# Handing two batches between DFT stages through DRAM in place of transposes on chip

## The chip, the cores and the metric

The kernel runs on one NeuronCore of one Trainium2 chip. The metric is the time of one execution on the device, in microseconds (us). The engines are PE (matmul), DVE (vector), ACT (scalar) and POOL (GpSimd); SP issues most DMAs and computes nothing. Each engine works through its own instructions in program order, and so does SP's DMA queue: an instruction that waits holds up everything behind it on its engine.

## What is computed

The reference mixes tokens with a filter in the frequency domain, and sends every token through one of eight two-layer experts, chosen by a hash of its id:

```python
# x: (8, 2496, 256) f32; filt_r, filt_i: (1249, 256)
X = np.fft.rfft(x, axis=1)
Y = X * (filt_r + 1j * filt_i)[None]
x = np.fft.irfft(Y, n=2496, axis=1).astype(np.float32).reshape(19968, 256)

expert_idx = token_ids * np.int64(2654435761) % np.int64(8)
for e in range(8):                       # w1: (8, 256, 1024), w2: (8, 1024, 256)
    mask = expert_idx == e
    out[mask] = np.maximum(x[mask] @ w1[e], 0.0) @ w2[e]
```

## The kernel before

**Two halves that overlap.** The eight batches go through a DFT written as matmuls, in three stages. The filtered tokens are scattered, row by row, to the table `xs` in DRAM, where each expert's tokens lie together in tiles of 256. The expert half then takes tile after tile from `xs`: `load` fetches one, `up` multiplies by `w1`, `down` by `w2`, and `store` scatters the results to the output. The tiles are ordered by the batches that they need. The first tiles hold tokens of batches 0 and 1 alone, so the expert half can begin when these two batches (`first` and `second` in the code) are in `xs`. All that is done ahead of the first tile is called the head here. The other six batches are worked in between the tiles.

**The three stages.** 2496 points are split into 39 x 64. `stage1` does the short DFT. `forward` and `back` are stage 2: `forward(u)` multiplies two of the 20 frequencies s by the table `d_t` on PE, and DVE applies the filter to the result (four passes, L318 to L323); `back(u)` multiplies by `e_t`. There are N_2 = 10 steps u. `stage3(u)` does the short inverse DFT for up to four columns j of the result (NU = 6 steps), has ACT copy the rows to a buffer `o`, and has POOL scatter them with one indirect DMA per column, 22 for each batch (L433). `room(u)` takes an `o` buffer and writes the token numbers into it on DVE; there are four such buffers for the first two batches, and one comes free when its scatters have landed.

**How data gets from stage to stage.** Stage 3 needs the data with other indices on the partitions than stage 2 leaves them. Batches 2 to 7 go through a tile in DRAM: `back` writes, `load4` reads. Batches 0 and 1 stay on chip. For them `back_c` takes the place of `back`: it exchanges the operands of the matmul, so that the result has channels on the partitions, kept in `self.out`. `turn4(u)` then transposes it with the identity matrix on PE (44 transposes for a batch, 84 of full size in both) into PSUM banks a to d, and ACT (first) or DVE (second) copies them to the tile `t4` that `stage3` reads. `t4` tiles come from a pool of two, eight columns each (index v = u // 2).

**Where things lie.** `self.out` of first is a part of `wts`, the buffer that later holds the weights of the expert tiles; `self.out` of second is a part of `mid`. The stage-1 results of fourth (batch 3) go to the same part of `mid`. `third` is batch 2. The tiles of x for stage 1 come from a pool of two, `xpool`.

**What sets the order.** The order of the head is written out by hand. `head` is a list of pairs (number, piece); sorted by the number, it gives the order in which the pieces are issued. The numbers resemble microseconds but act as keys only: each engine, and SP, receives its part of every piece in that order. In `chain(k)`, first's stage 2 runs as turn2 (towards stage 2), back and forward. Second's own steps of stage 2 have the keys 62.7 + 2.9 u. `weights(i, which)` loads the weights of tile i on SP, `load1` the x tiles, `load2` the inputs of stage 2. At its end, `begin()` frees the buffers of the head, and `load(0)` and `load(1)` fetch the first tiles; they wait for the scatters of batches 0 and 1. Fourth's first four steps of stage 1 have keys just below these (123 to 123.3).

The pieces' keys before, as far as the change touches them:

```python
    at = (63, 68.6, 74.4, 80.2, 86, 91)
    head += [(t, lambda u=u: first.turn4(u)) for u, t in enumerate(at)]
    head += [(t + 3, lambda u=u: first.stage3(u)) for u, t in enumerate(at)]
    head += [(96 + 5 * u - 4 * (u > 0), lambda u=u: second.turn4(u)) for u in range(NU)]
    head += [(98 + 5 * u, lambda u=u: second.stage3(u)) for u in range(NU)]
```

Of the kernel before, what the change touches and what calls it, by code (L numbers as in the profile page):

```python
# [19 lines left out]
P = 128  # L20
# [105 lines left out]
def kernel(  # L126
# [92 lines left out]
    class Batch:  # L219


        def __init__(self, b):
            self.b = b
            self.d1 = self.d2 = None
            self.x, self.t2, self.t4, self.p, self.o = {}, {}, {}, {}, {}
            self.g = None
            if b < 2:

                if b == 0:
                    own = mid[:, 0:5, :].rearrange("p k f -> p (k f)")  # L230
                    self.mixed = own.rearrange("p (h n s) -> p h n s", h=2, s=NS)
                after = (held[:, 0:NS * C] if b == 0 else mid[:, 5:10, :].rearrange("p k f -> p (k f)"))
                self.out = after.rearrange("p (h n s) -> p h n s", h=2, s=NS)

# [18 lines left out]
        def products(self, w, rows, cols, src, dst, copy, u, name):  # L253
# [3 lines left out]
            for i in range(1 if last else XG // 2):  # L257
                ps = fps.tile([P, 2, C], F32, name=f"{name}_{self.b}_{u}_{i}", tag="f")
                if last:
# [112 lines left out]

        def back_c(self, u):
            pr = self.p.pop(u)
            ps = fps.tile([P, 2, 2, P], F32, name=f"pc_{self.b}_{u}", tag="f")
            for i in range(2):
                for h in range(2):
                    nc.tensor.matmul(out=ps[:, i, h, :], lhsT=pr[:, i, h * P:(h + 1) * P],
                                     rhs=e_t[:, 2 * u + i, :], start=True, stop=True)
            nc.scalar.copy(out=self.out[:, :, :, 2 * u:2 * u + 2], in_=ps[:].rearrange("p i h n -> p h n i"))  # L380

        def turn4(self, u):
            v, j0 = divmod(XG * u, XL)
            if j0 == 0:
                self.t4[v] = t4pool.tile([NK, XL, C], F32, name=f"t4_{self.b}_{v}", tag="t4")
            copy = nc.vector.tensor_copy if self.b else nc.scalar.copy
            for k in range(0, min(XG, HN + 1 - XG * u), 2):
                tag = ("bc" if self.b and u % 2 else "ad")[k // 2]
                ps = banks[tag].tile([P, 2, C], F32, name=f"pu_{self.b}_{u}_{k}", tag=tag)
                rows = [2 * NS * (H if XG * u + k + i < HN else 1) for i in range(2)]  # L390
                for i in range(2):
                    n0 = 2 * H * (XG * u + k + i)
                    for h in range(2):
                        nc.tensor.transpose(out=ps[0:rows[i], i, h * P:(h + 1) * P],
                                            in_=self.out[:, h].rearrange("p n s -> p (n s)")[:, n0 * NS:n0 * NS + rows[i]],
                                            identity=ident[:])
                if rows[0] == rows[1]:
                    copy(out=self.t4[v][:, j0 + k:j0 + k + 2, :], in_=ps[0:NK])
                else:
                    for i in range(2):  # L400
                        copy(out=self.t4[v][0:rows[i], j0 + k + i, :], in_=ps[0:rows[i], i, :])

# [348 lines left out]
    def chain(k):  # L751

        for step, j in ((Batch.turn2, k + 1), (Batch.back_c, k - 2), (Batch.forward, k)):
            if 0 <= j < N_2:
# [23 lines left out]
    head += [(62.7 + 2.9 * u, lambda u=u: second.forward(u)) for u in range(N_2)]  # L778
    head += [(62.7 + 2.9 * (u + 2) - .1, lambda u=u: second.back_c(u)) for u in range(N_2)]
    at = (63, 68.6, 74.4, 80.2, 86, 91)  # L780
    head += [(t, lambda u=u: first.room(u)) for u, t in enumerate((60, 65, 71, 77, 83, 88.5))]
    head += [(t, lambda u=u: second.room(u)) for u, t in enumerate((92, 96.9, 101.9, 106.9, 111.9, 116.9))]
    head += [(t, lambda u=u: first.turn4(u)) for u, t in enumerate(at)]
    head += [(t + 3, lambda u=u: first.stage3(u)) for u, t in enumerate(at)]
    head += [(t, lambda v=v: third.load1(v)) for v, t in enumerate((72, 73, 74))]
    head += [(t, lambda k=k: weights(k // 2, k % 2)) for k, t in enumerate((95, 95.1, 95.2, 95.3))]
    head += [(96 + 5 * u - 4 * (u > 0), lambda u=u: second.turn4(u)) for u in range(NU)]
    head += [(98 + 5 * u, lambda u=u: second.stage3(u)) for u in range(NU)]
    head += [(99 + 5 * u - 3 * (u == 5), lambda u=u: third.stage1(u)) for u in range(NU)]
    head += [(123.5, lambda: begin()), (123.6, lambda: [load(i) for i in range(2)])]  # L790
# [340 lines left out]
```

## Time and profile before

| What | Value |
|---|---|
| time of the kernel, median of 3 runs (lowest, highest) | 1452.11 us (1450.68, 1458.1) |
| the profiled execution: its time, its span | 1424.24 us, 1422.5 us |
| its mean granted PE clock | 0.99 |
| busy over the span: PE, DVE, ACT, POOL | 97%, 63%, 29%, 58% |
| first matmul of the first expert tile (`up_a`) starts at | 141.85 us |
| scatters of first and second start, from the first to the last | 69.97 us to 135.26 us |
| bytes moved by DMA over the span | 278.33 MB |

The profile is of one execution, which was shorter than the timed runs; times within the kernel are measured from the start of its span. A line of the timeline gives start, duration, engine, line, operation, output <- input, the count of merged instructions, and in brackets how long the engine was idle before and what ended that. A line of the chain of waits gives start, duration, and what that stretch was spent in. Lines of the code are named by L and their number; a line of a helper stands for all who call it, so L267 is the matmuls of stages 1 (`pa`) and 3 (`pd`), and L433 is every scatter to `xs`. In names, `pc` is the result of `back`, `pb` of `forward`, `pu` of `turn4`.

In the head the engines are less full than over the span. In the windows of the trace, from 60 to 80 us PE is busy 15.91 us, DVE 15.76, ACT 7.26 and POOL 5.92; from 100 to 120 us PE 19.22, DVE 6.89, ACT 10.03 and POOL 15.07. The DMA engines' share is 0.66 and 0.95.

### The profile page before, as it was taken

The numbers are of one execution on the slowest core, as the hardware profiler recorded it, in microseconds if no ns is written. First come the engines' busy times: TensorE is split into PE (matmuls) and PEld (weight loads), VectorE is DVE, ScalarE is ACT, GpSimd is POOL, SyncE is SP. The second block draws the span as 40 slices with busy tenths as digits, with TensorE's granted clock in tenths as the row PEclk, the third lists the DMA queues.
The fourth block names the chain that finished last, engine by engine and source line by source line (L and its number), as shares of the span: only waits on it lengthen the run. The fifth ranks groups of instructions, "written<-read, shape, count | busy, mean of one in ns | idle before, by whom it ended". The sixth has DMA issues, their size and how long they took to land.

```text
span 1422.5 us, 26307 instructions
## 1 busy us (share of the span) xinstructions
PE 1373.4 (97%) x9398; PEld 1273.3 (90%) x9398; DVE 890.2 (63%) x1636; ACT 416.6 (29%) x760; POOL 830.3 (58%) x736
## 2 busy tenths in 40 slices
PE   7898999999999999999999999999999999999997
PEld 7776888989888988889999899999999999999997
DVE  7773575575556566445665477657766776676775
ACT  4554122223232223232222222222222222222222
POOL 6167243844665565578533587788855566555563
PEclk9999899999999999999999999999999999999999
DMA  8677765757987698888755785887742526261611
GB/s 222 206 235 216 212 218 121 260 192 245 269 270 224 183 284 264 261 262 273 241 167 131 219 258 170 235 242 235 254 138 68 190 62 199 46 218 42 215 46 35
DMA packets 244505, 278.33 MB, mean 196 GB/s; under 512 B 125171, under 2 KB 213670, under 8 KB 234948
## 3 DMA queue, kind: packets, MB, share of 16 engines
q1 hardware_dynamic: 95149, 179.33, 40.2%
q10 hardware_dynamic: 129303, 52.69, 15.4%
q0 software_dynamic: 19920, 44.59, 8.9%
q8 instruction: 77, 1.26, 0.4%
q14 instruction: 56, 0.46, 0.1%
HBM read 293.65 MB, written 86.15 MB: 267 GB/s over the span
## 4 chain that ended last, share of the span: by engine, by line
PE 86%; DMA 8%; DVE 3%; issue 1%; ACT 1%; ACTq 0%; SPq 0%; POOLq 0%; POOL 0%; DVEq 0%
PE dps L922 22%; PE up_b L887 9%; PE up_a L887 6%; PE up_c L887 6%; PE pd L267 5%; PE pb L312 4%; PE dnc L949 4%; PE dnb L949 4%; PE dna L949 4%; PE upc L944 4%; PE upa L944 4%; PE pc L335 3%; PE pa L267 3%; DMA t<-d 2%; PE upe L944 2%; PE upb L944 2%
## 5 line engine op out<-in xcount | busy, mean ns | idle before, releaser
L922 PE MATMUL dps<-wts,ht 128*128 128x256 f32 x1600 | 370.9, 382 | 6.1 <-ACT ht L891 6.1
L922 PEld LDWEIGHTS dps<-wts,ht 128*128 128x128 f32 x1600 | 304.7, 192 | 50.6 <-ACT ht L891 7.3
L1014 POOL DMA_INDIRECT out_dram<-osb,no x158 | 165.2, 1046 | 219.2 <-DVE osb L956 137.8
L433 POOL DMA_INDIRECT xs<-o,sidx x176 | 177.0, 1006 | 168.7 <-ACT o L269 73.3
L877 POOL TENSOR_TENSOR tw<-wts 128x512 f32<-128x512 f32 x158 | 205.1, 1298 | 116.0 <-DMA wts<-in_moe_w_dram 92.4
L877 POOL TENSOR_TENSOR tw<-wts,tw 128x512 f32<-128x512 f32 x158 | 206.1, 1305 | 6.2
L894 DVE TENSOR_TENSOR ht<-up_b,ht 128x512 f32<-128x512 f32 x150 | 103.7, 691 | 114.6 <-PE up_b L887 91.2
L891 ACT ACTIVATE ht<-ht 128x512 f32<-128x512 f32 x150 | 94.3, 630 | 188.8 <-DVE ht L894 164.9
L322 DVE TENSOR_TENSOR z<-pb,filt 64x512 f32<-64x512 f32 x160 | 110.2, 689 | 30.9 <-PE pc L335 28.9
L927 DVE COPY osb<-dps 128x512 f32<-128x512 f32 x50 | 34.6, 691 | 150.2 <-PE dps L922 149.7
L887 PE MATMUL up_a<-xt,wts 128*128 128x128 f32 x800 | 115.3, 277 | 9.1 <-DVE xt L855 4.9
L887 PEld LDWEIGHTS up_a<-xt,wts 128*128 128x128 f32 x800 | 105.9, 193 | 12.7 <-DVE xt L855 5.3
L887 PE MATMUL up_b<-st,tw 128*128 128x128 f32 x800 | 107.4, 278 | 2.7 <-DVE ht L894 1.8
L887 PEld LDWEIGHTS up_b<-st,tw 128*128 128x128 f32 x800 | 98.1, 193 | 4.9 <-issue 3.7
L953 ACT ACTIVATE ht<-ht 128x512 f32<-128x512 f32 x90 | 56.6, 630 | 122.1 <-DVE ht L956 75.8
L894 DVE TENSOR_TENSOR ht<-up_c,ht 128x512 f32<-128x512 f32 x100 | 69.0, 690 | 37.2 <-PE up_c L887 32.4
L338 ACT COPY mid<-pc 128x512 f32<-128x512 f32 x60 | 35.0, 584 | 154.8 <-PE pc L335 91.5
L267 PE MATMUL pd<-t,wi_t 120*117 120x256 f32 x320 | 77.5, 385 | 2.6 <-DMA t<-d 2.6
L318 DVE TENSOR_TENSOR y<-pb,filt 128x512 f32<-128x512 f32 x80 | 55.1, 689 | 37.8 <-PE pb L312 35.6
L269 ACT COPY o<-pd 117x512 f32<-117x512 f32 x80 | 45.0, 585 | 104.4 <-DMA xg<-xs 45.4
L312 PE MATMUL pb<-mid,d_t 128*128 128x256 f32 x280 | 74.1, 388 | 1.1 <-DVE z L322 1.1
L898 ACT COPY ht<-up_a 128x512 f32<-128x512 f32 x50 | 29.3, 587 | 150.6 <-PE up_a L887 120.7
(210 smaller groups left out, 2466.1 us busy)
## 6 DMA issues: line engine op xcount, KB each, us to landing
wts<-in_moe_w_dram SPq DMA_DIRECT2D x162, 1024.0 KB
xg<-xs ACTq DMA_DIRECT2D x321, 64.0 KB
mid<-d SPq DMA_DIRECT2D x70, 256.0 KB
d<-mid ACTq DMA_DIRECT2D x60, 256.0 KB
d_t<-t2s SPq DMA_DIRECT2D x15, 1024.0 KB
e_t<-t2s SPq DMA_DIRECT2D x15, 1024.0 KB
x<-in_x_dram SPq DMA_DIRECT2D x39, 312.0 KB
t<-d SPq DMA_DIRECT2D x12, 960.0 KB
```

Of the source, the lines that this page charges most:

```text
L267: nc.tensor.matmul(out=ps[0:cols * H, k, :], lhsT=w[:], rhs=src[:, 2 * i + k, :], start=True, stop=True)
L312: nc.tensor.matmul(out=ps[:, i, :], lhsT=d_t[:, s, :], rhs=rhs, start=True, stop=True)
L322: nc.vector.tensor_tensor(out=z[b], in0=ps[a], in1=f_t[1][64 * hi:64 * hi + 64, s1:s1 + 2, :], op=OP.mult)
L433: st = nc.gpsimd.indirect_dma_start(out=xs[:], out_offset=bass.IndirectOffsetOnAxis(ap=index, axis=0), in_=rows, in_offset=None, bounds_ch ...
L877: eng.tensor_tensor(t[k][:], p, q, op=OP.subtract)
L887: nc.tensor.matmul(out=ps[bank][:, f, :], lhsT=w[:, f * P:(f + 1) * P], rhs=xx, start=first and f == 0, stop=True, skip_group_check=True)
L891: nc.scalar.activation(out=out, in_=in_, func=AF.Relu)
L894: nc.vector.tensor_tensor(out, ps[bank][:], other, op=OP.add)
L922: nc.tensor.matmul(out=ps[:, h, :], lhsT=ht[:, h, fp, :], rhs=w2[:, fp, :], start=(fp == 0), stop=(fp == FP - 1))
L944: nc.tensor.matmul(out=ps[:, f, :], lhsT=w[:, f * P:(f + 1) * P], rhs=xx, start=first and f == 0, stop=True, skip_group_check=True)
L949: nc.tensor.matmul(out=ps[:, 0, :], lhsT=a[:, f, :], rhs=b[:, f, :], start=first and f == 0, stop=True, skip_group_check=True)
L1014: st = nc.gpsimd.indirect_dma_start(out=out[:], out_offset=bass.IndirectOffsetOnAxis(ap=to_rows[i][:, h:h + 1], axis=0), in_=o[:, h, :], i ...
```

## The change

For first and second, `turn4` and its transposes go. `back_on_chip` takes the place of `back_c`: it multiplies in the other order, so that `self.out` has the 128 points on the partitions and lies as (s, c). `put(k)` writes four of the 20 values of s (512 KB) to a tile in DRAM as soon as they are there, in five puts for each batch. `fetch(v)` reads back eight columns j, in rows of 1 KB, with (x, s) on 120 partitions, to the `t4` tile that stage 3 reads; v = 2 is shorter and has a second small DMA. Both are issued on SP. Stage 3 of these two batches writes to the PSUM banks a to d that the transposes used.

The keys of the pieces around it change too. Second's stage 3 gets the keys 97 + 4.1 u, first's 67 + 4.4 u. The loads of third's x move to 49.5 to 54.6, the weights of tile 0 to 80, those of tile 1 to 102.2, and the loads of fourth's x to 103. Third's stage 1 moves to 89.5 to 102, and fourth's four steps of stage 1 go between second's steps of stage 3 (106 + 4.1 u).

```diff
-                self.out = after.rearrange("p (h n s) -> p h n s", h=2, s=NS)
+                self.out = after.rearrange("p (s c) -> p s c", c=C)
...
-                ps = fps.tile([P, 2, C], F32, name=f"{name}_{self.b}_{u}_{i}", tag="f")
+                tag = ("bc" if u % 2 else "ad")[i] if name == "pd" and self.b < 2 else "f"
+                ps = (fps if tag == "f" else banks[tag]).tile([P, 2, C], F32, name=f"{name}_{self.b}_{u}_{i}", tag=tag)
...
-        def back_c(self, u):
+        def back_on_chip(self, u):
             pr = self.p.pop(u)
-            ps = fps.tile([P, 2, 2, P], F32, name=f"pc_{self.b}_{u}", tag="f")
+            ps = fps.tile([P, 2, C], F32, name=f"pc_{self.b}_{u}", tag="f")
             for i in range(2):
-                for h in range(2):
-                    nc.tensor.matmul(out=ps[:, i, h, :], lhsT=pr[:, i, h * P:(h + 1) * P],
-                                     rhs=e_t[:, 2 * u + i, :], start=True, stop=True)
-            nc.scalar.copy(out=self.out[:, :, :, 2 * u:2 * u + 2], in_=ps[:].rearrange("p i h n -> p h n i"))
-
-        def turn4(self, u):
...
+                nc.tensor.matmul(out=ps[:, i, :], lhsT=e_t[:, 2 * u + i, :], rhs=pr[:, i, :], start=True, stop=True)
+            nc.scalar.copy(out=self.out[:, 2 * u:2 * u + 2, :], in_=ps[:])
+
+        def put(self, k):
+
+            if self.d2 is None:
+                self.d2 = dpool.tile([P, NS, C], F32, name=f"d2_{self.b}", tag="d2")
+            sl = slice(SG * k, SG * k + SG)
+            nc.sync.dma_start(out=self.d2[:, sl, :], in_=self.out[:, sl, :])
+
+        def fetch(self, v):
+            t4 = self.t4[v] = t4pool.tile([NK, XL, C], F32, name=f"t4_{self.b}_{v}", tag="t4")
+            n = min(XL, HN - XL * v)
+            main = self.d2[0:2 * H * HN].rearrange("(j x) s c -> (x s) j c", x=2 * H)
+            nc.sync.dma_start(out=t4[:, 0:n, :], in_=main[:, XL * v:XL * v + n, :])
+            if n < XL:
+                nc.sync.dma_start(out=t4[0:2 * NS, n, :], in_=self.d2[2 * H * HN:P].rearrange("x s c -> (x s) c"))
...
-    head += [(62.7 + 2.9 * (u + 2) - .1, lambda u=u: second.back_c(u)) for u in range(N_2)]
-    at = (63, 68.6, 74.4, 80.2, 86, 91)
-    head += [(t, lambda u=u: first.room(u)) for u, t in enumerate((60, 65, 71, 77, 83, 88.5))]
-    head += [(t, lambda u=u: second.room(u)) for u, t in enumerate((92, 96.9, 101.9, 106.9, 111.9, 116.9))]
-    head += [(t, lambda u=u: first.turn4(u)) for u, t in enumerate(at)]
-    head += [(t + 3, lambda u=u: first.stage3(u)) for u, t in enumerate(at)]
-    head += [(t, lambda v=v: third.load1(v)) for v, t in enumerate((72, 73, 74))]
-    head += [(t, lambda k=k: weights(k // 2, k % 2)) for k, t in enumerate((95, 95.1, 95.2, 95.3))]
-    head += [(96 + 5 * u - 4 * (u > 0), lambda u=u: second.turn4(u)) for u in range(NU)]
-    head += [(98 + 5 * u, lambda u=u: second.stage3(u)) for u in range(NU)]
-    head += [(99 + 5 * u - 3 * (u == 5), lambda u=u: third.stage1(u)) for u in range(NU)]
+    head += [(62.7 + 2.9 * (u + 2) - .1, lambda u=u: second.back_on_chip(u)) for u in range(N_2)]
+    head += [(65.5 + 4.4 * u, lambda u=u: first.room(u)) for u in range(NU)]
+    head += [(67 + 4.4 * u, lambda u=u: first.stage3(u)) for u in range(NU)]
+    head += [(t, lambda v=v: first.fetch(v)) for v, t in enumerate((62.66, 62.67, 72))]
+    head += [(23 + 3.6 * (2 * k + 3) + .05, lambda k=k: first.put(k)) for k in range(NS // SG)]
+    head += [(t, lambda v=v: third.load1(v)) for v, t in enumerate((49.5, 54.5, 54.6))]
+    head += [(t, lambda k=k: weights(k // 2, k % 2)) for k, t in enumerate((80, 80.1, 102.2, 102.3))]
+    head += [(95.5 + 4.1 * u, lambda u=u: second.room(u)) for u in range(NU)]
+    head += [(97 + 4.1 * u, lambda u=u: second.stage3(u)) for u in range(NU)]
+    head += [(t, lambda v=v: second.fetch(v)) for v, t in enumerate((94.56, 94.57, 102))]
+    head += [(62.7 + 2.9 * (2 * k + 3) - .05, lambda k=k: second.put(k)) for k in range(NS // SG)]
+    head += [(t, lambda u=u: third.stage1(u)) for u, t in enumerate((89.5, 92, 94.6, 95, 98, 102))]
...
-    head += [(t, lambda v=v: fourth.load1(v)) for v, t in enumerate((113, 113.1))]
-    head += [(123 + .1 * u, lambda u=u: fourth.stage1(u)) for u in range(4)]
+    head += [(t, lambda v=v: fourth.load1(v)) for v, t in enumerate((103, 103.1))]
+    head += [(106 + 4.1 * u, lambda u=u: fourth.stage1(u)) for u in range(4)]
```

More of the change, by code (lines that the diff above doesn't have):

```diff
@@ L382, in turn4 @@
-        def turn4(self, u):
[L383 to L401, printed above, removed]
@@ L751, in chain @@
     def chain(k):
-        for step, j in ((Batch.turn2, k + 1), (Batch.back_c, k - 2), (Batch.forward, k)):
+        for step, j in ((Batch.turn2, k + 1), (Batch.back_on_chip, k - 2), (Batch.forward, k)):
             if 0 <= j < N_2:
```

## The prediction

> **What bounds the kernel now.** I read the page's busy shares first, then the chain that ended last, then the timeline of POOL and SP in the head, and last the windows of DMA traffic.
>
> ```profile
> PE 1373.4 (97%) x9398; PEld 1273.3 (90%) x9398; DVE 890.2 (63%) x1636; ACT 416.6 (29%) x760; POOL 830.3 (58%) x736
> ```
>
> PE is 97% busy over the span; from 180 us on it is busy 1218.8 of 1242 us. The change leaves that part alone, so the answer is one number: how much earlier or later the first expert tile starts (first `up_a`, 141.85 us). The chain says what releases it:
>
> ```profile
> 120.97 0.29 issue
> 121.26 0.12 POOL xs L433
> 121.38 1.17 issue
> 122.55 3.72 DMA xs<-o,sidx
> ...
> 126.99 1.21 PE pd L261 x4
> 128.20 8.80 PE pa L267 x32
> ...
> 138.46 2.31 DMA xg<-xs
> ...
> 141.85 1.22 PE up_a L887 x4
> ```
>
> The 8.80 us of `pa` are fourth's stage 1, which looks like PE as the bound. The reader should not stop there. The timeline of POOL has the scatters that `load(0)` must wait for:
>
> ```profile
> 69.97 1.10 POOL L433 DMA_INDIRECT xs<-o,sidx  x1 [22.66 <-DVE o L412]
> 71.37 1.02 POOL L433 DMA_INDIRECT xs<-o,sidx  x1 [0.30 <-issue]
> ...
> 104.44 0.90 POOL L433 DMA_INDIRECT xs<-o,sidx  x1 [0.30 <-issue]
> 105.70 0.99 POOL L433 DMA_INDIRECT xs<-o,sidx  x1 [0.36 <-ACT o L269]
> ...
> 135.26 0.90 POOL L433 DMA_INDIRECT xs<-o,sidx  x1 [0.30 <-ACT mid L269]
> 137.90 1.26 POOL L877 TENSOR_TENSOR tw<-wts 128x512 f32<-128x512 f32 x1 [1.74 <-DMA xs<-o,sidx]
> ```
>
> A scatter is 0.99 us and the next starts 0.30 us after it: 1.30 us each, 5.2 us for a stage-3 step of four. First's 22 end at 105.3, second's follow at once, and the last starts at 135.26: from 97.78 on POOL has only one gap over 0.4 us (2.55 us before 126.09). The last scatter starts 6.6 us before `up_a`; the `pa` beside it end at 137.0 and are cover. So in the head's second half **POOL is the bound**: 44 x 1.30 = 57.2 us from the first scatter, plus POOL's idle gaps.
>
> SP's queue and the DMA at the first crossing:
>
> ```profile
> 59.31 13.33 SPq L303 DMA_DIRECT2D mid<-d  x10
> 72.68 7.19 SPq L249 DMA_DIRECT2D x<-in_x_dram  x9
> ```
>
> ```profile
> 62.00:64.00 2.00, 1.23 (x8) 1.26 (x9) 0.70 (x2) 0.00 (x0) 0.00 (x0) 0.83 0.87 277
> 64.00:66.00 2.00, 2.00 (x7) 1.53 (x7) 0.00 (x0) 0.69 (x1) 0.00 (x0) 0.50 0.89 285
> 68.00:70.00 2.00, 2.00 (x12) 1.72 (x11) 1.80 (x9) 0.67 (x3) 0.03 (x1) 1.00 0.09 31
> ```
>
> (Window, length, busy PE, PEld, DVE, ACT, POOL, clock, DMA share, GB/s.) Second's load2 fills the DMA at about 285 GB/s from 61 to 68 us.
>
> **What the Trainium skill says.** "DMA: Bandwidth & Descriptors", section "Anatomy of one DMA — SWDGE (gpsimd) path": a semaphore wait is taken on the issuing sequencer before dispatch, and about 2 us of each DMA are fixed, mostly the write receipt. The trace agrees: SP shows such waits, and a 26 KB load lands after 2.4 us. Its section "Queues, rings and completion order": on one engine descriptors of a ring are consumed in order; a transfer queued on SP goes behind SP's earlier ones. No row shows that directly. "Perfetto Trace Analysis", "DMA Instruction — SWDGE (GPSIMD)": a POOL DMA's bar is descriptor generation. It agrees: 1.0 us on POOL, landing after 5.3 us (median). "TensorE: Matmul & The Clock Gate", Part 1: an idle window halves PE's clock. It agrees: 0.50 at 64 to 66 us after the pauses around 60.
>
> **The change, part by part.**
>
> *Steps with one answer.* back_on_chip: 4 PE instructions of 217 ns (the chain's `pb` x4, same shape, 0.87 us) against 8 of 111 ns (`pc` x8, 0.89 us): nothing. Its copy is contiguous: 584 ns (L338) for 690 (L380), 2.1 us of ACT in 20, hidden, since ACT is busy half of the time. Stage 3's other PSUM banks: nothing. turn4 goes: 88 transposes by 109 ns (the chain's `pu` x8, 0.87 us) are 9.6 us of PE; ACT loses 5 x 1.07 + 0.63 = 6.0 us, DVE 5 x 1.29 + 0.74 = 7.2. What is late next is POOL's scatters, so these buy nothing of themselves while scatters are the limit. fourth's four stage1 steps move from the end to between second's stage3 steps: they lay beside scatters 128.7 to 136.2, so taking them from the end gains nothing either.
>
> *First crossing.* First's out is complete at 65.0 (copy of 64.35). Then it must be put, land, be fetched, land; before, the transposes read it on chip and stage 3 began at 68.0. SP works in order: put 0 to 2 early, third.load1(0), then eight load2 that wait for d1 (59.0 now), then third.load1(1) and (2), and only then puts 3 and 4 and fetch 0. I take d1 1.5 us later, since puts and load1(0) (1.5 MB) now share the DMA with d<-mid: load2 from 60.8. Issue alone: 8 x 0.58 + 6 x 0.75 + 2 x 0.5 = 10.2 us, so put 4 goes out at 71. Bytes ahead of its end: load2 2.10 + load1 1.68 + puts 1.05 = 4.83 MB; at 310 GB/s (load2's 2.1 MB took 6.8 us) 15.6 us, from 62.6 (1.8 us from issue to data): 78.2, landed 79. Fetch 0 (0.98 MB, 3.2 us) with 1.8 us ahead: 84. PE meets stage3(0) after forward(1), near 69, and waits, with back(0) and forward(2) behind it; DVE runs dry with them. Stage 3 starts at 83.5, 15.5 us late. Bounds: with an idle DMA, 3.5 us for a 0.5 MB put (d<-mid's 0.64 MB took 4.3 from issue to release) and 5 for the fetch give 74; with every transfer at 260 GB/s, 87.
>
> *From there to second's out.* PE restarts slow (1 us): first scatter at 86.5, first's 22 done at 115. forward(2) reaches DVE 5 us after stage3(0), 88.5; eight forwards by 2.76 us plus 1.9 of experts and rooms end at 112.5, back and copy at 114. (Before: 72.75 to 101.9, 29 us; the missing transposes give back 4.)
>
> *Second crossing.* SP is free, but put 4 and fetch are serial: 0.5 + 3.5 + 5.5 = 9.5, second's stage3(0) at 123.5. third.stage1(2) and (3), 3.5 us, cover a part. POOL idles 115 to 126. Then 21 intervals of 1.30: last scatter's start 153.3, against 135.26: +18.
>
> *SP behind second's fetch.* fetch(2) waits for a t4 buffer, thus for stage3(1), about 129.5; weights(1) (2.1 MB) and fourth.load1(0) (0.96 MB) queue behind it, 3.7 MB in all at about 310: x lands near 144. fourth.stage1(0) stands before stage3(3) in PE's order, and POOL has eaten steps 0 to 2 at 141.6. Its next scatter comes at 147: 0 to 6 us of idling. I take 4.
>
> Moved at nothing: third.load1(0) (DMA share is 0.49 at 50 to 60), weights(0) (2.1 MB beside scatters; without room it delays second's put 4 by up to 7 us).
>
> Sum: 18 + 4 = **+22 us** on the profiled execution's 1424.24 (span 1422.5). The timed runs' median, 1452.11, stands 28 us above that execution; the head's waits are of DMA and POOL, so I carry the difference over unscaled: **1474 us**.
>
> **Rivals.**
> - *Light crossings* (20%). The DMA swallows SP's backlog; fetch 0 lands at 75. For it: a DMA share of 0.09 at 68 to 70. Against: 4.8 MB in order. Then first scatter 77.5, second's out at 105, stage 3 at 114.5, last scatter 143.8: +8.5, 1460.
> - *The crossing is hidden; not slower* (10%). Mechanism: with PE and DVE freed, POOL never idles after the first scatter, and its 10.3 us of gaps in the head go. Place: the two waits at stage3(0). It decides if fetch 0 lands by 72 and second's stage3(0) comes within 28.6 us of first's. Price: first scatter 74, the last 43 intervals of 1.30 later, 129.9: -5, 1447. Against: even an idle DMA gives 74, and from stage3(0) over DVE's eight forwards and a round trip it is 39 us.
> - *Pile-up* (17%). weights(0), puts, scatters and fourth's x collide at the second crossing as well: 10 us more, +32, 1484. For it: 13 us from issue to release for one d<-mid at 112 to 125.
>
> **How the numbers follow.** Forecast 53%, own range +14 to +30 (1466 to 1482). A measurement here tells about 0.5%, 7.3 us, from no change. The range holding 8 in 10 takes in most of the light crossings and the near pile-up: 1457 to 1486. Slower: 53 + 17 + 16 of the light ones, 86; same: 4 of these and 3 of the hidden one, 7; faster: 7.
>
> **What would show it.** Right: SP's first fetch issues after 76, PE waits over 10 us for `t<-d` near 69 to 84, POOL's first scatter after 82, a POOL pause of 6 us or more between the batches, scatters still 1.30 us apart, first `up_a` near 164. Wrong: fetch 0 issued by 68 with puts landed, or scatters closer than 1.2 us, or `up_a` before 150.

## The result

The changed kernel takes 1505.47 us, median of 5 runs (1503.62 to 1513.87), against 1455.78 for the kernel before (5 runs, 1450.68 to 1465.71) on the same chip: a ratio of 1.0357, 95% interval 1.0325 to 1.0389. It is slower by 50 us; the forecast was slower by 22, and the range ended at 1486. All ratios below are to the kernel before on the same chip; from chip to chip that kernel took 1420 to 1459 us (medians), so absolute times are compared only between runs on chips where it takes about as long.

### The profile page after: what moved, and what is told of

Read it like the earlier page. It is cut to its first block, busy times and chain, and to the rows that moved or that the text cites. A ratio compares the mean times of both kernels' runs of the same rounds, so it can differ in the third digit from the quotient of the medians.

```text
span 1512.1 us, 25952 instructions
## 1 busy us (share of the span) xinstructions
PE 1385.2 (92%) x9230; PEld 1274.5 (84%) x9230; DVE 866.5 (57%) x1624; ACT 407.2 (27%) x748; POOL 826.7 (55%) x736
## 4 chain that ended last, share of the span: by engine, by line
PE 72%; DMA 12%; issue 7%; DVE 4%; POOL 2%; SPq 1%; ACT 1%; another core or an unknown queue 1%; ACTq 1%; POOLq 0%; DVEq 0%
PE dps L916 17%; PE up_b L881 8%; PE up_a L881 5%; PE up_c L881 5%; PE dnc L943 4%; PE dna L943 4%; PE dnb L943 4%; PE upc L938 3%; PE upa L938 3%; PE pd L268 3%; PE pb L313 3%; DMA d<-mid 3%; PE pc L336 3%; DMA xg<-xs 2%; PE pa L268 2%
## 5 line engine op out<-in xcount | busy, mean ns | idle before, releaser
L268 PE MATMUL pd<-t,wi_t 120*117 120x256 f32 x320 | 81.0, 397 | 36.4 <-DMA t<-d 34.8
L268 PEld LDWEIGHTS pd<-t,wi_t 120*117 120x117 f32 x320 | 59.6, 190 | 50.3 <-issue 20.6
L268 PE MATMUL pa<-x,wf_t 117*120 117x256 f32 x264 | 68.5, 406 | 24.9 <-DMA x<-in_x_dram 20.6
L268 PEld LDWEIGHTS pa<-x,wf_t 117*120 117x120 f32 x264 | 50.9, 196 | 37.2 <-issue 23.8
```

What stands on the lines that cost most here:

```text
L268: nc.tensor.matmul(out=ps[0:cols * H, k, :], lhsT=w[:], rhs=src[:, 2 * i + k, :], start=True, stop=True)
```

## The profile after

The profiled execution took 1513.87 us (span 1512.1). The busy times of its page, to be held against those of before:

```profile
PE 1385.2 (92%) x9230; PEld 1274.5 (84%) x9230; DVE 866.5 (57%) x1624; ACT 407.2 (27%) x748; POOL 826.7 (55%) x736
```

PE has 168 instructions less (88 transposes, and 80 by the other order of `back`), yet PE is busy for 92% of the span where it was 97%. PE doesn't have more to do: it waits. The timeline of POOL says where (start, duration, engine, line, what, and in brackets the idle time before and what ended it):

```profile
96.23 1.10 POOL L426 DMA_INDIRECT xs<-o,sidx  x1 [46.41 <-ACT o L270]
97.63 1.02 POOL L426 DMA_INDIRECT xs<-o,sidx  x1 [0.30 <-issue]
...
129.72 0.90 POOL L426 DMA_INDIRECT xs<-o,sidx  x1 [0.30 <-DVE z L323]
151.51 0.99 POOL L426 DMA_INDIRECT xs<-o,sidx  x1 [20.90 <-ACT o L270]
...
165.75 0.99 POOL L426 DMA_INDIRECT xs<-o,sidx  x1 [0.30 <-issue]
181.56 0.99 POOL L426 DMA_INDIRECT xs<-o,sidx  x1 [14.82 <-ACT o L270]
...
193.19 0.90 POOL L426 DMA_INDIRECT xs<-o,sidx  x1 [0.30 <-issue]
```

Scatters are still 0.99 us with 0.30 between. But the first comes 26.3 us later (69.97 before), between the batches POOL now idles 20.90 us, and a pause of 14.82 us lies in second's batch. First `up_a` follows the last scatter by 6.7 us as before (6.6), at 199.93 instead of 141.85; the chain of waits has no more between them than the scatter's landing and the load of the tile:

```profile
191.91 2.72 DMA xs<-o,sidx
...
196.39 2.65 DMA xg<-xs
...
199.93 2.09 PE up_a L881 x8
```

PE's timeline gives what each of the three holes waits for:

```profile
93.26 3.73 PE L268 MATMUL pd<-t,wi_t 120*117 120x256 f32 x8 [19.95 <-DMA t<-d]
...
101.83 1.89 PE L268 MATMUL pd<-t,wi_t 120*117 120x256 f32 x8
...
148.54 3.76 PE L268 MATMUL pd<-t,wi_t 120*117 120x256 f32 x8 [11.62 <-DMA t<-d]
...
175.19 3.74 PE L268 MATMUL pa<-x,wf_t 117*120 117x256 f32 x8 [15.84 <-DMA x<-in_x_dram]
```

Two holes are the fetch from DRAM (`t<-d`), one for each batch; the third is fourth's x. Eight matmuls take 3.7 us after each of them and 1.89 otherwise: PE restarts at half the clock, as "TensorE: Matmul & The Clock Gate" of the Trainium skill, Part 1, has it for idle windows.

SP's timeline shows the queue behind these waits (a merged line counts the waits within it):

```profile
66.40 4.98 SPq L304 DMA_DIRECT2D mid<-d  x8
71.42 4.79 SPq L249 DMA_DIRECT2D x<-in_x_dram  x6
76.32 0.93 SPq L386 DMA_DIRECT2D d<-wts  x2
85.33 0.95 SPq L392 DMA_DIRECT2D t<-d  x2
...
141.00 15.79 SPq L392 DMA_DIRECT2D t<-d  x3
156.84 0.47 SPq L394 DMA_DIRECT2D t<-d  x1
160.01 1.61 SPq L457 DMA_DIRECT2D wts<-in_moe_w_dram  x2
163.00 0.01 SPq L460 DMA_DIRECT2D wts<-in_moe_w_dram  x1
163.02 4.81 SPq L249 DMA_DIRECT2D x<-in_x_dram  x6
```

Second's eight load2, then third's x, and only then first's last two puts (`d<-wts`) and fetch 0, in the order that the prediction described; load2 starts at 66.40 where 60.8 was forecast. The chain of waits joins the pieces at the first crossing:

```profile
76.32 0.46 SPq L386
76.78 0.06 issue
76.89 8.29 DMA d<-wts
85.33 7.80 DMA t<-d
93.13 0.14 issue
93.26 3.73 PE pd L268 x8
```

8.29 us for a put of 512 KB, then 7.80 for the fetch. The windows of the DMA between them (last three numbers: PE clock, DMA share, GB/s):

```profile
82.00:84.00 2.00, 0.00 (x0) 0.00 (x0) 0.00 (x0) 0.00 (x0) 0.00 (x0) 0.50 0.73 300
84.00:86.00 2.00, 0.00 (x0) 0.00 (x0) 0.00 (x0) 0.00 (x0) 0.00 (x0) 0.50 0.05 18
86.00:88.00 2.00, 0.00 (x0) 0.00 (x0) 0.00 (x0) 0.00 (x0) 0.00 (x0) 0.50 0.50 96
88.00:90.00 2.00, 0.00 (x0) 0.00 (x0) 0.00 (x0) 0.00 (x0) 0.00 (x0) 0.50 0.96 227
90.00:92.00 2.00, 0.00 (x0) 0.00 (x0) 0.00 (x0) 0.00 (x0) 0.00 (x0) 0.50 1.12 212
```

At 84 to 86 the DMA engines are all but empty: the put's last bytes are through, but it counts as landed only at 85.18, and the fetch, issued at 85.33, isn't moving yet. Then the fetch runs at 212 to 227 GB/s at a DMA share of 0.96 to 1.12.

Part of the 58 us is the chip: before's profile was taken on one where it needs 1424 us. k_before_again, the kernel before on a chip where it takes 1452.33, starts `up_a` at 151.16; set against that the profile after is 49 us later. g_after, the changed kernel on a chip where the kernel before takes 1423.22, is the fairer row (first `up_a` 195.32, and +57 us in the whole time):

| stretch | forecast | profile after | g_after |
|---|---|---|---|
| start to first scatter | +16.5 | +26.3 | +26.5 |
| to second's first scatter | +3.8 | +19.6 | +14.6 |
| to second's last scatter | +1.7 | +12.1 | +12.8 |
| to first `up_a` | 0 | +0.1 | -0.4 |
| sum | +22 | +58.1 | +53.5 |

(us against before's profile; g_after's scatters start at 96.49, 146.78 and 189.10. In the profile after, one wait of 2.77 us at 124.88 is put down to "another core or an unknown queue"; g_after has no such wait and a second stretch shorter by 5 us; it isn't explained.)

The prediction took all that follows `up_a` to stay as it was. On quick chips, where the kernel before takes 1420 to 1424 us, it did: from there to the end of the span it is 1280.7 us before, 1284.2 in g_after and 1279.5 in e_both below. On slower ones (1452 to 1459 us) it is 1293.2 in k_before_again, but 1307.5 to 1312.2 in three kernels with the new order (j_no_dram, v_e_again, after). These are single executions; what is lost there wasn't followed.

## The experiments

**What do the transposes cost, and does the result repeat?** d_no_transposes is the kernel before without its 88 transposes (84 of full size); the copies to `t4` stay.

```diff
-                    for h in range(2):
-                        nc.tensor.transpose(out=ps[0:rows[i], i, h * P:(h + 1) * P],
...
-                    copy(out=self.t4[v][:, j0 + k:j0 + k + 2, :], in_=ps[0:NK])
+                        copy(out=self.t4[v][0:r, j0 + k + i:j0 + k + i + w, :],
+                             in_=self.out.rearrange("p h n s -> p (h n s)")[0:r, 0:w * C].rearrange("p (w c) -> p w c", c=C))
```

> The kernel before with the transposes of turn4 left out: ACT or DVE copies a piece of self.out to t4 instead, in the same number of copies, so stage 3 works on untransposed values. It gives the 9.6 us of PE of the 88 transposes and costs no hand-over. Theory 1 (POOL's scatters bound the head): up_a 1 to 5 us before the 141.9 of the kernel before, from POOL's gaps in first's part alone. Rival (PE bounds the head): up_a 8 to 10 us before it.

Measured: 1417.32 us for 1420.38, ratio 0.9978 (0.9959 to 0.9996); first `up_a` at 139.40, 2.4 us earlier. POOL scatters back to back from 78.91 on, and `up_a` follows its last scatter by 6.8 us:

```profile
132.58 0.90 POOL L427 DMA_INDIRECT xs<-o,sidx  x1 [0.30 <-issue]
139.40 2.08 PE L881 MATMUL up_a<-xt,wts 128*128 128x128 f32 x8 [5.41 <-DVE xt L849]
```

So the transposes, with nothing to pay for their absence, are worth 0.2%: the change had next to nothing to win on PE. (The copies to `t4`, which the change removes too, stay in this run; no run leaves them out alone.)

> The changed kernel itself once more, beside the others on one chip. Both theories: first scatter 96, second's first scatter 151, first up_a 200, each within 3 us; the time over the kernel before is 45 to 60 us.

Measured: 1480.3 us for 1423.22, ratio 1.0384 (1.0335 to 1.0432). The result repeats.

**SP's order at each crossing.** a_load1_late moves third's x behind first's puts and first two fetches; b_x4_early moves fourth's x ahead of second's fetch 2 and of weights(1); e_both does both.

```diff
-    head += [(t, lambda v=v: third.load1(v)) for v, t in enumerate((49.5, 54.5, 54.6))]
+    head += [(t, lambda v=v: third.load1(v)) for v, t in enumerate((62.68, 62.69, 62.695))]
...
-    head += [(t, lambda v=v: fourth.load1(v)) for v, t in enumerate((103, 103.1))]
+    head += [(t, lambda v=v: fourth.load1(v)) for v, t in enumerate((95.1, 95.2))]
```

> The changed kernel with third's three x loads issued on SP after first's fetches 0 and 1 (keys 62.68 to 62.695 in place of 49.5, 54.5, 54.6). Theory 1 (the head waits for hand-overs in SP's order, and POOL's 1.30 us scatters then run from there): puts 3 and 4 no longer stand behind six x loads (4.8 us of issue, 1.7 MB), d1 of second lands 2 to 4 us sooner, so the first scatter comes 8 to 12 us before 96.2 and the first up_a 5 to 12 us before 199.9. Theory 2 (the added bytes load the DMA engines, in whatever order): same bytes, so first scatter and up_a within 3 us of the changed kernel's.

> The changed kernel with fourth's x loads issued on SP before second's fetch 2 and the weights of tile 1 (keys 95.1, 95.2 in place of 103, 103.1). Theory 1: the pause of POOL in the middle of second's scatters (14.8 us, 166.7 to 181.6) goes to under 3 us, and up_a comes 11 to 14 us before 199.9; the start of second's stage 3 moves by less than 3. Theory 2: same bytes, up_a within 3 us of 199.9.

> The changed kernel with both moves on SP: third's x after first's fetches, and fourth's x before second's fetch 2. Theory (two separate queues of bytes in SP's order): the gains of the two single moves add up, 15.7 + 18.9 = 35 us, up_a at 163 to 168 in place of 199.9, so still 21 to 26 us behind the kernel before: what stays are the two round trips themselves. Rival (the two moves gain the same wait once): up_a at 177 or later.

| run | ratio (95% interval) | first scatter | second's first | pause in second | `up_a` |
|---|---|---|---|---|---|
| g_after | 1.0384 (1.0335, 1.0432) | 96.49 | 146.78 | 15.46 | 195.32 |
| a_load1_late | 1.0321 (1.0271, 1.0371) | 84.51 | 135.69 | 14.84 | 184.18 |
| b_x4_early | 1.0310 (1.0249, 1.037) | 96.00 | 146.61 | 0.48 | 181.00 |
| e_both | 1.0217 (1.0159, 1.0275) | 86.40 | 137.21 | 0.67 | 171.43 |

(g_after and e_both ran on one chip; a_load1_late, b_x4_early and c_fetch_from_x below on another, where the kernel before takes 1420.38 us for 1423.22.) The two parts are separate and nearly add up: 11.1 and 14.3 alone, 23.9 together. e_both missed its forecast of 163 to 168 for `up_a`: that was reckoned from the first profile of after (199.93), and the same kernel on this chip starts at 195.32. In a_load1_late load2 starts at 60.70, near the 60.8 of the prediction, but third's x doesn't explain all of the delay: in the eight runs that have these loads late load2 starts at 60.70 to 65.06 (62.7 on the mean), in the four that have them early at 65.58 to 67.41 (66.4), before at 59.31, and in j_no_dram below, without puts and with x late, at 58.59. Of the 7.1 us about half goes with third's x, and half with the puts. In b_x4_early second's scatters run through: the pause was fourth's x alone. POOL in e_both:

```profile
137.21 0.99 POOL L426 DMA_INDIRECT xs<-o,sidx  x1 [18.33 <-ACT o L270]
138.51 0.99 POOL L426 DMA_INDIRECT xs<-o,sidx  x1 [0.30 <-issue]
...
164.86 0.89 POOL L426 DMA_INDIRECT xs<-o,sidx  x1 [0.30 <-issue]
```

Only the wait between the batches is left (18.33 us), and the late first scatter; e_both is slower than the kernel before by 2.2%.

**The fetch's wait for the puts.** c_fetch_from_x (on after) and h_both_no_wait (on e_both) read the same shape from x, so no fetch waits for a put.

```diff
-            main = self.d2[0:2 * H * HN].rearrange("(j x) s c -> (x s) j c", x=2 * H)
+            d2 = bass.AP(tensor=x.tensor, offset=x.offset, ap=[[NS * C, P], [C, NS], [1, C]])
+            main = d2[0:2 * H * HN].rearrange("(j x) s c -> (x s) j c", x=2 * H)
```

> The changed kernel with fetch reading the same shape from the input x in place of the tile that put writes, so that no fetch waits for a put; bytes and order on SP are as in the changed kernel, and the values are not those of the reference. Theory 1: fetch 0 follows put 4 on SP at once (77 and 135 in place of 85.3 and 141.0): first scatter 5 to 8 us sooner, second's another 5 to 7, up_a 10 to 15 us before 199.9. Theory 2: up_a within 3 us of 199.9.

> As e_both, with fetch reading the same shape from the input x in place of the put's tile, so that no fetch waits for a put; the values are not those of the reference. c_fetch_from_x gained only 1 us at the first crossing. Theory A (there, load1's and the puts' bytes stood in front of the fetch in SP's queue, so the wait was not what held it; with them out of the way it is the wait): the pause of the DMA engines between the puts' last byte and the fetch's first (3 us in e_both, at both crossings) goes, first scatter at 82 to 84 in place of 86.4, up_a 5 to 9 us before e_both's 171.4. Theory B (the wait costs nothing in any order): within 2 us of e_both. Either way up_a stays over 15 us behind the kernel before, since put bytes and fetch bytes still come one after the other.

c_fetch_from_x was a miss: first scatter at 95.57, only 0.9 us earlier than g_after, `up_a` at 189.01, 6.3 earlier; ratio 1.0337 (1.0297 to 1.0377). SP and PE show why: the fetch goes out 5.6 us earlier than in g_after (85.51) and is in use only 0.9 us earlier, since load2, third's x and the puts are ahead of it:

```profile
77.50 1.61 SPq L386 DMA_DIRECT2D d<-wts  x2
79.90 3.52 SPq L393 DMA_DIRECT2D t<-in_x_dram  x2
```

```profile
92.60 3.60 PE L268 MATMUL pd<-t,wi_t 120*117 120x256 f32 x8 [17.28 <-DMA t<-in_x_dram]
```

This agrees with the ring that is worked off in order, which "DMA: Bandwidth & Descriptors" of the Trainium skill ("Queues, rings and completion order") describes and of which no row of before had shown anything: 12.7 us from issue to use here, 7.9 in the kernel after. With the backlog gone (h_both_no_wait) the wait for the put counts: stage 3 begins at 79.07 instead of e_both's 83.41, the first scatter comes at 82.06 instead of 86.40, and the hole in the DMA is closed:

```profile
72.00:74.00 2.00, 0.00 (x0) 0.00 (x0) 1.94 (x4) 0.00 (x0) 0.00 (x0) 0.50 0.98 350
74.00:76.00 2.00, 0.00 (x0) 0.00 (x0) 0.84 (x2) 0.00 (x0) 0.00 (x0) 0.50 1.05 231
76.00:78.00 2.00, 0.00 (x0) 0.00 (x0) 0.00 (x0) 0.00 (x0) 0.00 (x0) 0.50 1.05 228
```

Its ratio, 1.0169 (1.0127 to 1.0211), isn't separated from e_both's. It ran on a slower chip than e_both; the first crossing shows little of that (first scatter of the changed kernel at 96.23 and 96.49 on two chips, of e_both's at 86.40 and 86.01), but its later times, `up_a` at 172.97 among them, are not set beside e_both's.

**Short rows?** f_long_rows is e_both with the fetch reading as many bytes in rows of 8 KB, in the wrong order.

```diff
-            main = self.d2[0:2 * H * HN].rearrange("(j x) s c -> (x s) j c", x=2 * H)
-            nc.sync.dma_start(out=t4[:, 0:n, :], in_=main[:, XL * v:XL * v + n, :])
+            main = self.d2[:].rearrange("x s c -> (x s) c")[0:NK * n].rearrange("(p j) c -> p j c", j=n)
+            nc.sync.dma_start(out=t4[:, 0:n, :], in_=main)
```

> As e_both, and fetch reads the same number of bytes from the same tile as rows of 8 KB (6 KB) in place of 1 KB pieces, so the columns reach stage 3 in a wrong order; puts and their waits stay. Theory (fetch is slow since 1 KB pieces move at about 200 GB/s with full DMA engines): fetch to first matmul falls from 7.7 to about 5.5 us, at both crossings, and up_a comes 3 to 6 us before e_both's. Rival (fetch is all latency): within 1 us of e_both.

Measured: ratio 1.0236 (1.0185 to 1.0288), `up_a` at 170.08 for 171.43. From its issue to stage 3's first matmul the fetch takes 7.0 and 7.3 us at the two crossings, for 7.6 and 7.8 in e_both, at 217 to 250 GB/s for 201 to 226. The row size makes 0.6 us of it at most; the 2 us that the theory expected aren't there.

**Why does a put take 8 us?** Two transfers lie beside the last puts. At the second crossing ACT issues third's first stage-1 result 1.5 us ahead of second's last put. The DMA traffic of after from 133 to 141 us, by queue (packets, MB, share):

```profile
q10 hardware_dynamic: 975, 0.98, 52.5%
q1 hardware_dynamic: 144, 0.52, 18.5%
```

Two thirds of what moves there aren't the put. At the first crossing second's load2 stand ahead of it. s_d1_behind takes away the one (SP issues it behind fetches 0 and 1), t_load2_behind the other (four of the eight load2 go behind fetch 0), u_all_behind both; v_e_again is e_both beside them.

```diff
-    put_off = {2: [], 3: []}
+    put_off = {2: [], 3: [], 4: []}
...
-                if (self.b == 2 and v > 0) or (self.b == 3 and v < 2):
-                    put_off[self.b].extend(moves)
+                if (self.b == 2) or (self.b == 3 and v < 2):
+                    put_off[4 if self.b == 2 and v == 0 else self.b].extend(moves)
...
+    head += [(94.6, lambda: [nc.sync.dma_start(out=dram, in_=chip) for dram, chip in put_off[4]])]
```

```diff
-    head += [(t, lambda g=g: second.load2(g)) for g, t in enumerate((54, 54.1, 54.2, 54.3, 70))]
+    head += [(t, lambda g=g: second.load2(g)) for g, t in enumerate((54, 54.1, 62.665, 62.666, 70))]
```

> e_both once more, unchanged, as the base for the three beside it on one chip. Both theories: second's last put to the issue of second's first fetch 7 to 8.5 us, first's the same, up_a within 2 us of the 171.4 of e_both if the chip is alike.

> e_both, with one transfer moved: third's first stage-1 result (0.98 MB, issued by ACT 1.0 us ahead of second's last put) is issued by SP behind second's fetches 0 and 1 instead. Theory 'shared DMA': of the 7.9 us that second's last put (0.52 MB) takes there until the fetch is issued, about 3.5 are third's bytes, so it falls to 4 to 5 us; second's first scatter and up_a come 3 to 4 us earlier. Rival 'own latency': a put takes 7 to 8 us whatever lies beside it; within 1 us of e_both. Rival 'moved': the bytes now lie beside the fetch, which takes 2 to 4 us longer; up_a within 1 us.

> e_both, with four of second's eight load2 transfers (1.05 MB of 2.10 MB), which stand ahead of first's last two puts on SP, moved behind fetch 0. Theory 'shared DMA': 2.5 us of issue and 3 us of bytes less ahead of the last put, fetch 0 is issued 3 to 5 us earlier, and first scatter and up_a come 3 to 5 us earlier. Rival 'own latency': issue to landing of the put stays at 7 us, the fetch comes 2.5 us earlier by the issue time alone. Rival 'moved': the loads are late for second's forward(4), the gain at the first scatter is lost by second's first scatter.

> Both of these moves together. Theory 'shared DMA': they add up, up_a 6 to 8 us earlier than e_both, time 0.4 to 0.5% lower; still slower than before by 1.5 to 2%, since two fetches of 7.7 us and two puts of 4 remain. Rival 'own latency': 3 us at most.

| run | ratio (95% interval) | first: put, fetch | second: put, fetch | first scatter | second's first | `up_a` |
|---|---|---|---|---|---|---|
| v_e_again | 1.0267 (1.022, 1.0314) | 6.8, 7.7 | 6.9, 7.9 | 86.01 | 140.97 | 179.02 |
| s_d1_behind | 1.0227 (1.0181, 1.0273) | 6.9, 7.7 | 2.5, 7.9 | 88.11 | 137.38 | 177.08 |
| t_load2_behind | 1.0264 (1.0214, 1.0315) | 3.4, 7.5 | 6.9, 7.7 | 81.66 | 137.50 | 174.88 |
| u_all_behind | 1.0218 (1.0171, 1.0266) | 4.1, 7.5 | 2.5, 7.6 | 84.93 | 135.16 | 172.92 |

(put: from the end of its issue on SP to the issue of fetch 0; fetch: from that to stage 3's first matmul. v_e_again is the kernel of e_both, whose `up_a` was at 171.43 on its chip; here the kernel before takes 1454.68 us.) The second crossing on SP, first v_e_again, then s_d1_behind:

```profile
104.61 18.61 SPq L386 DMA_DIRECT2D d<-mid  x3
130.13 0.94 SPq L392 DMA_DIRECT2D t<-d  x2
```

```profile
106.01 17.99 SPq L386 DMA_DIRECT2D d<-mid  x3
126.48 0.94 SPq L392 DMA_DIRECT2D t<-d  x2
127.47 1.83 SPq L784 DMA_DIRECT2D d<-mid  x1
```

The last put ends its issue at 123.22 in the one and at 124.00 in the other, and the fetch goes out 6.9 and 2.5 us later. Each crossing answers to its own neighbour and not to the other's. With its neighbour gone, second's put takes 2.5 us; first's, with half of load2 still ahead of it, 3.4 and 4.1. The rest of the 6.8 and 6.9 us belonged to the transfers that were moved. The fetch doesn't answer to any of this. The time follows in part: u_all_behind starts `up_a` 6.1 us earlier than v_e_again and its median is 5.8 us lower (1485.99 for 1491.78), s_d1_behind's 4.6 lower; t_load2_behind's is 1.2 lower, although its `up_a` comes 4.1 us earlier, so what it loses later wasn't followed. s_d1_behind gives back at two pauses within second (3.33 and 2.97 us) part of the 4.4 us won. The intervals of these four ratios overlap; what is said of the crossings rests on the traces.

**The new order without the change, and the change without DRAM.** p_moves_alone is the kernel before, transposes kept, with the new keys of third's x, third's stage 1, weights(1) and fourth's x; in r_moves_no_x third's x is back at 72 to 74.

```diff
-    head += [(t, lambda v=v: third.load1(v)) for v, t in enumerate((72, 73, 74))]
-    head += [(t, lambda k=k: weights(k // 2, k % 2)) for k, t in enumerate((95, 95.1, 95.2, 95.3))]
+    head += [(t, lambda v=v: third.load1(v)) for v, t in enumerate((49.5, 54.5, 54.6))]
+    head += [(t, lambda k=k: weights(k // 2, k % 2)) for k, t in enumerate((95, 95.1, 102.2, 102.3))]
...
-    head += [(99 + 5 * u - 3 * (u == 5), lambda u=u: third.stage1(u)) for u in range(NU)]
+    head += [(t, lambda u=u: third.stage1(u)) for u, t in enumerate((89.5, 92, 94.6, 95, 98, 102))]
...
-    head += [(t, lambda v=v: fourth.load1(v)) for v, t in enumerate((113, 113.1))]
+    head += [(t, lambda v=v: fourth.load1(v)) for v, t in enumerate((103, 103.1))]
```

> The kernel before, transposes and all, with the new keys of third's x loads (49.5 to 54.6), third's stage 1 (89.5 to 102), the weights of tile 1 (102.2) and fourth's x (103), no data through DRAM. Theory (the crossings cost, the moves cost only through what waits behind them on SP): up_a within 4 us of 141.9. Rival (the new order costs by itself): up_a over 10 us later.

> As p_moves_alone, with third's x loads back at their keys of before (72, 73, 74); third's stage 1, the weights of tile 1 and fourth's x stay at their new keys. Theory (in p_moves_alone six x loads stood on SP in front of second's load2(4), which ACT's copies of second's stage 2 wait for, 7.3 us): the first long pause of POOL (8.0 us) falls back to about 3, and up_a is 4 to 9 us before p_moves_alone's 152.7. Rival (the new places of stage 1 and weights cost): up_a within 3 us of 152.7.

p_moves_alone missed its forecast (within 4 us of before): it is slower by 0.6% (1.0060, 1.0036 to 1.0083), and `up_a` starts at 152.69 in its profile, which is of its longest execution (1443.53 us, median 1431.91). r_moves_no_x isn't slower (0.9993, 0.9973 to 1.0013). POOL's first long pause in it is 3.01 us for 8.02, as expected; its `up_a` isn't, at 161.74, on a chip where the kernel before takes 1459.46 us and has no profile to compare with. So of these four moves only that of third's x costs anything that the times show, about 9 us of 1423. The other new keys of the changed kernel (the weights of tile 0, the steps of stage 3, fourth's stage 1) weren't tried in the kernel before.

j_no_dram is e_both with puts and fetches left out and third's x at 72 to 74; in their place ACT (first) and DVE (second) copy parts of `self.out` to `t4` ahead of each stage-3 step. k_before_again is the kernel before, on the same chip.

```diff
-            nc.sync.dma_start(out=self.d2[:, sl, :], in_=self.out[:, sl, :])
+            pass
...
-            nc.sync.dma_start(out=t4[:, 0:n, :], in_=main[:, XL * v:XL * v + n, :])
+            pass
...
+                    copy(out=self.t4[v][0:rows[k + i], j0 + k + i:j0 + k + i + w, :],
+                         in_=flat[0:rows[k + i], (NS - w) * C:].rearrange("p (w c) -> p w c", c=C))
```

> As e_both with put and fetch left out: ACT (first) or DVE (second) copies a piece of self.out to t4 just before each stage 3, so stage 3 works on wrong values; third's x loads stand at the keys of before (72 to 74), all else in the changed order. Theory (what keeps e_both 29 us behind are the two trips through DRAM): first scatter at 69 to 72, second's first within 3 us of POOL's end with first's, up_a within 5 us of that of the kernel before on this chip. Rival (the changed order or back_on_chip costs by itself): up_a over 10 us behind it.

> The kernel before once more with a profile, beside j_no_dram on one chip: up_a at 140 to 146 on a quick chip, later on a slow one; ratio 1 within its interval.

`up_a` starts at 148.36 in j_no_dram and at 151.16 in k_before_again; first scatter 68.76 and 70.23, second's first 112.91 and 111.22. Without the trips through DRAM the head is as short as before on this chip, so the trips, with what they wait for and drag along, are what e_both loses up to `up_a`. Inside, the two heads differ: between the batches POOL still pauses for 9.32 us in j_no_dram (4.55 in k_before_again, 18.33 in e_both), so about half of that pause is the new order and not the trip; and in k_before_again `up_a` comes 8.7 us after the last scatter, where its chain of waits runs through fourth's stage 1. The whole time of j_no_dram is 0.4% longer all the same (1.0037, 1.0018 to 1.0057); what it loses behind `up_a` wasn't followed.

**A try at the kernel before.** q_gap moves third's last two stage1 steps behind second's last stage 3, to close the pause of 2.55 us at 126.09.

```diff
-    head += [(99 + 5 * u - 3 * (u == 5), lambda u=u: third.stage1(u)) for u in range(NU)]
+    head += [(t, lambda u=u: third.stage1(u)) for u, t in enumerate((99, 104, 109, 114, 123.01, 123.02))]
```

> The kernel before with third's last two steps of stage 1 moved behind second's last stage 3 (keys 123.01, 123.02 in place of 119, 121). In the kernel before POOL pauses 2.5 us before 126.1, when ACT waits for third's d1 store to land before it may write mid again. If POOL's scatters bound the head, that pause goes and up_a comes 1.5 to 2.5 us earlier, about 0.15% of the time, hardly to be told apart in the times; if not, up_a stays within 0.5 us of 141.9.

Measured: ratio 1.0011 (0.9992 to 1.003), no gain. The trace doesn't show what the pause was worth. There is one of 2.55 us at 126.52, but ahead of second's ninth scatter and ended by a copy to `o`; the one aimed at stood ahead of the fifteenth and was ended by a copy to `mid`, and k_before_again, on another of the slower chips, doesn't have it either. And `up_a` missed both forecasts: it starts at 160.27, 16.6 us after the last scatter, because the stage-1 steps on PE now end at 154.90 and the first tile's load comes behind them. No version found here beats the kernel before.

## Why the forecast was right in kind and wrong in size

For the start of `up_a` the forecast of +22 us is 31.5 short of g_after, which ran on a chip as quick as that of before's profile: 10.0 up to the first scatter, 10.8 from there to second's first, 11.1 within second, -0.4 behind it. (In the profile after it is 36.1: 9.8, 15.8, 10.4 and 0.1.) The places were right and the sizes of four terms were not: the late load2 and fetch at the first crossing, third's stage 1 in second's stage 2, put and fetch at the second crossing, and the wait for fourth's x.

- **The bound.** Right. POOL's scatters set the head, the transposes were worth 2.4 us of `up_a` (d_no_transposes), and their going bought nothing. Only in the kernel before and two variants of it on slower chips did `up_a` come more than 7.1 us after the last scatter (k_before_again 8.7, q_gap 16.6, r_moves_no_x 17.6); the account of the head holds for quick chips and for the new order.
- **The order on SP at the first crossing.** Right: load2, third's x, the last two puts, fetch 0. The term "d1 1.5 us later" failed: load2 started at 66.40, 7.1 us later than before, about half of it with third's x and half with the puts.
- **Put 4 to stage3(0), "landed 79", "84".** The put was issued 5.8 us later than forecast (76.8 for 71) and took the 8 us that were forecast; the fetch took 7.9 us from issue to use where 5 were put down. In sum stage3(0) at 93.26 for 83.5, and the first scatter 9.7 us later than forecast.
- **From stage3(0) to second's out, 83.5 to 114.** 30.5 us were forecast; g_after takes 33.7. The forecast counts DVE's forwards and puts nothing down for third's stage 1, whose new keys 89.5 and 92 stand ahead of second's last `back` (94.5), so that PE works on it first (g_after):

```profile
121.03 1.99 PE L268 MATMUL pa<-x,wf_t 117*120 117x256 f32 x8
122.86 1.03 PE L378 MATMUL pc<-y,e_t 128*128 128x256 f32 x4
123.72 1.89 PE L268 MATMUL pa<-x,wf_t 117*120 117x256 f32 x8
125.45 1.03 PE L378 MATMUL pc<-y,e_t 128*128 128x256 f32 x4
```

That is read from the trace; no run moves these steps. The profile after takes 40.8 us, and all runs on slower chips 38.5 to 41.0 where those on quick ones take 33.3 to 35.6; what they wait for wasn't followed.

- **Second crossing, "0.5 + 3.5 + 5.5 = 9.5".** Wrong in itself: 16.6 us in g_after (copy's end at 127.23, stage 3 at 143.81) and 14.5 in the profile after. Near 3.5 us is right for a put alone (2.5 in s_d1_behind), but it took 8.2 in g_after: third's stage 1, of which the forecast counted two steps as cover, puts 0.98 MB on the DMA just ahead of it. The fetch took 8.1 for 5.5, and 7.5 to 8.1 in every variant in which it waits for the puts and reads rows of 1 KB. The prediction took the fetch from bytes at the rate that load2 shows (about 300 GB/s); it ran at 200 to 230.
- **Fourth's x, "0 to 6 us of idling. I take 4."** Right in place and cause (fetch 2, then weights(1), then x, on one queue), wrong in size: 14.82 us, where the forecast's own steps give 5.4 (147 less 141.6). From fetch 2 to the use of x it was 18.7 us for 14.5, although the DMA moved 314 to 393 GB/s from 164 to 172 us: the x loads went out only 6.5 us behind fetch 2, since SP stood at the weights. From x to the next scatter it was 6.4 us for 3, with PE at half the clock. b_x4_early removes the wait by changing two keys.
- **"Moved at nothing": weights(0) and third.load1(0).** Not so for third's x: its loads alone cost 0.6% in the kernel before (p_moves_alone against r_moves_no_x), in part because load1(1) and (2) stand ahead of second's last load2 on SP. weights(0) wasn't tried alone; it is issued at 110.54 and second's last put over 23 us later.
- **The signs.** All that were to show that it is right came true but the last: `up_a` near 164.
- **The rivals.** "Light crossings" and "hidden" fell: fetch 0 was issued at 85.33, not landed by 75. "Pile-up" named the mechanism of a part of the missing time, bytes that collide at the second crossing, but not third's stage-1 result among them, and was still 18 us too small.
- **Two slips in the sums.** Fetch 0 is landed at 84 and stage 3 begins at 83.5; the steps of the light crossings give 144.3 for the last scatter, not 143.8. Neither matters here.

In one sentence: three waits were foreseen in their places, and each was priced as if its transfer had SP and the DMA nearly to itself, while what the change had moved next to them (third's x, third's stage 1) was put down as nothing or as cover. What stays open: why the fetch runs at 200 to 230 GB/s, the wait of 2.77 us at 124.88, and what slower chips lose in second's stage 2 and behind `up_a`.

## What to carry to other kernels

A hand-over through DRAM costs a put and a fetch in series. Here a put of 512 KB took 2.5 us without its neighbour and 6.6 to 8.3 us with other transfers just ahead of it, and a fetch of 960 KB 7.0 to 8.1 us whatever was moved away; price both on the path of the engine that sets the end, and not by the matmuls that it saves. Where a load sits behind a fetch on the same queue, it inherits the fetch's wait: moving fourth's x ahead of it was worth 14 us. Before an operation is replaced, leave it out once: the transposes were worth 0.2%.

## What was not expected of the hardware

- Once under way, the fetch to 120 partitions runs at 198 to 250 GB/s with the DMA engines' share at 0.92 to 1.12, with rows of 1 KB and of 8 KB, from the tile in DRAM and from x alike; a window with puts and second's load2 in h_both_no_wait (70 to 72 us) has 418 GB/s at a share of 1.04.
- Between a put's last bytes and a dependent fetch's first ones the DMA is all but empty for 2 to 3 us (18 GB/s at 84 to 86 us in the profile after); without the wait the gap is gone (h_both_no_wait).
- After a wait PE runs a whole stage-3 step at half the clock: 3.5 to 3.8 us for 1.9 after all its waits for data of 7.6 us and more, and 3.60 after one of 4.09 us (u_all_behind); after 0.5 us it is 1.96 (b_x4_early).
